# Issuing more of a routed-expert kernel's list loads from GpSimd: 239 of its transfers in place of 211

## The chip, the cores and the metric

The kernel runs on one core of a Trainium2 chip. A core has a matrix engine (PE in the profile, its weight loads PEld), a vector engine (DVE), a scalar engine (ACT), a general-purpose engine (GpSimd, POOL in the profile) and a sync engine (SP) that only issues transfers. Each engine has its own queue of instructions and runs it in order; engines meet at semaphores. Transfers (DMAs) are issued by SP, ACT or GpSimd, and all share 16 DMA engines. Those issued by SP and ACT appear in the profile as "hardware dynamic", those issued by GpSimd as "software dynamic".

The metric is the device time of one execution in microseconds (us). The median of three runs before the change is 696.01 us, with 694.29 and 697.36 at the ends.

## What is computed

The first half is a gated linear recurrence over 768 steps for 4 x 8 heads of size 48. Its result, 3072 rows of 384 numbers, is the input of the second half, a mixture of 8 experts in which every row goes to the two experts with the highest noisy score. Everything is 32-bit floating point.

```python
for t in range(S):
    state = alpha[:, :, t, :, None] * state + np.einsum('bhd,bhe->bhde', k[:, :, t], v[:, :, t])
    y[:, :, t] = np.einsum('bhd,bhde->bhe', q[:, :, t], state)
...
noisy_logits = logits + noise_scale * noise
top2 = np.argpartition(-noisy_logits, 2, axis=1)[:, :2]
...
for e in range(E):
    for k in range(2):
        mask = top2[:, k] == e
        h = np.maximum(x[mask] @ w1[e], 0.0)
        out[mask] += top2_w[mask, k, None] * (h @ w2[e])
```

## The kernel before

**Recurrence.** It is done in 24 chunks of 128 steps with matmuls and scans. Each chunk's rows go to a table `x_rows` in device memory (`put_rows`). Beside the chunks and, later, beside the first expert tiles, a routing takes place in four units of six chunks: it picks the two experts of each row and writes one list entry of four words for each choice into a `table` in device memory: row number, gate, the other expert, and the rank in the other expert's list. An entry of expert e with rank r lies in row e * 3072 + r. The entries are written by 48 indirect transfers issued by GpSimd (`put_entries`, L161), 12 for each unit.

**Expert tiles.** Rows are then worked off in 24 pairs of 128-row tiles (`pairs`), and three half tiles of 64 rows (`half_tiles`). Pairs 0 to 7 are the first 256 entries of the experts 0 to 7; pairs 8 to 23 are the second and third 256 entries, two pairs for an expert, from expert 7 down. Pairs are multiplied with a seven-product scheme in place of eight products; the sums that it needs are made by DVE. For each pair there are these steps:

- `load_tab`: the 256 list entries, 4 KB as 256 runs of 16 bytes, into `tab` (6 buffers). Line 1017 decides who issues it: SP for pairs 0 to 13, GpSimd from pair 14 on (`PLANNED` = 14). From pair 14 on the place of the list in the table is read from a `plan` that the routing's last steps compute (`of_plan`).
- `load_w1`, `load_w2`: 1.5 MB each, only where the expert is new; issued by SP.
- `find_rows` (DVE) turns the entries into row numbers, `gather` (GpSimd, L886, two indirect transfers) brings the rows of `x_rows`, `turn_x` transposes them.
- `get_prev` (GpSimd, L871, two indirect transfers) brings what an earlier tile has written for the same rows to the output; it waits for all earlier output writes. `combine` (DVE, L1155) adds, and `put_pair` (GpSimd, L879, two indirect transfers) writes the output.

A half tile has the same steps with one indirect transfer each; `load(j)` (L1260) reads its place from the plan, loads its 64 entries through SP (L1263) and then both weights.

`take_tile` makes a list load wait for the entries that it may read: those of the first two units for pairs 0 to 7, all 48 writes for later pairs and half tiles.

**Order.** There is no scheduler: `steps(i)` gives every step of pair i a time on a common axis on which a pair takes 20 units, and the list of all steps is sorted by it and emitted in that order, for every engine. On this axis `load_tab(i)` lies at 20i - 32, `find_rows` at 20i - 27, `gather` at 20i - 26, `get_prev` at 20i + 8.5, `combine` at 20i + 20.9 and `put_pair` at 20i + 22.2; a half tile's `load` lies 48 units before its base. So `load_tab(i)` stands, on the queue of whoever issues it, just ahead of `get_prev(i-2)`. The entries' writes of the last unit end at 126.3.

**Transfers of GpSimd before.** 48 entry writes, 48 gathers, 48 loads and 48 writes of earlier output for pairs, 9 for half tiles, and 10 list loads: 211. A transfer of 128 rows is spread over the 16 DMA engines, 8 rows on each; a list load of a pair puts 16 runs on each, one of a half tile's transfers 4. Completion of each transfer is counted on one of eight semaphores that GpSimd's transfers take in turn; SP's take turns over eight others.

**End.** After the last output write, branches on two counts skip code for rare cases (L1406 and L1408), GpSimd waits for its transfers, and the program ends with a drain of every engine (line 1443, the end of the launch).

Of the kernel before, what the change touches and what calls it, by code (L numbers as in the profile page):

```python
# [9 lines left out]
F32 = mybir.dt.float32  # L10
# [8 lines left out]
def kernel(  # L19
# [32 lines left out]
    nc = tc.nc  # L52
    B, H, S, D = q.shape
    N, DM = out.shape
    E, _, F = moe_w1.shape
    C = 128
# [8 lines left out]
    NU = NT // UC  # L65
    LEVELS = [1 << i for i in range(C.bit_length() - 1)]
    HC = C // 2
# [5 lines left out]
    TROWS = E * RMAX + (E + 0) * C  # L73
# [3 lines left out]
    R2 = 2 * C  # L77
# [68 lines left out]
    table = dram.tile([TROWS, 4], U32, name="table")  # L146
# [22 lines left out]
    def take_tile(get, units=NU):  # L169
        count = 1 + 2 * UT // C * units  # L170
        for put in entries[:count]:
            tc.add_manual_dep(get.ins, put.name, AFTER, reason="reads any row of the table that these fill")
        for put in entries[count:]:
            tc.declare_no_dep(get.ins, put, reason="rows behind those of the tile")
        taken.append(get.ins)
# [694 lines left out]
    def get_rows(rows, at):  # L870
        get = nc.gpsimd.indirect_dma_start(out=rows.bitcast(U32), out_offset=None, in_=out.bitcast(U32),  # L871
                                           in_offset=bass.IndirectOffsetOnAxis(ap=at, axis=0),
                                           bounds_check=N - 1, oob_is_err=False)
        for put in order["puts"]:
            tc.add_manual_dep(get.ins, put.name, AFTER, reason="reads rows of any earlier tile")
        order["gets"].append(get.ins)
# [8 lines left out]
    def get_x(rows, at, units):  # L885
        nc.gpsimd.indirect_dma_start(out=rows, out_offset=None, in_=x_rows[0:units * UT, :],  # L886
                                     in_offset=bass.IndirectOffsetOnAxis(ap=at, axis=0),
                                     bounds_check=units * UT - 1, oob_is_err=False)

    def of_plan(i, what, most, engine=mybir.EngineType.SP):  # L890
        return nc.values_load(plan[0:1, i, what:what + 1], engines=[engine], min_val=0, max_val=most,
                              skip_runtime_bounds_check_because=WHY)

    def load_weights(e, w1, w2):
        if w1 is not None:
            nc.sync.dma_start(out=w1, in_=moe_w1[ds(e, 1)].rearrange("o (a p) f -> p (o a) f", p=C))
        if w2 is not None:
            nc.sync.dma_start(out=w2, in_=moe_w2[ds(e, 1)].rearrange("o (a p) d -> p (o a) d", p=C))

    def choose_rows(on, tab, where, i):  # L900

        R = tab.shape[0]
        skip, second, before_it = tab[:, 4:6], tab[:, 6:7], tab[:, 7:8]
        other = on["two"].tile([C, E], F32, name="other")[0:R]
        nc.vector.scalar_tensor_tensor(other, expert_ids[0:R], tab[:, 2:3], given[0:R, i, 0:E], op0=ALU.is_equal,
                                       op1=ALU.mult, accum_out=before_it)
        nc.vector.memset(skip[:, 0:1], 0.0)
        nc.vector.tensor_tensor(skip[:, 1:2], tab[:, 3:4], before_it, op=ALU.is_ge)
        nc.vector.tensor_tensor(second, tab[:, 3:4], before_it, op=ALU.is_lt)
        nc.vector.scalar_tensor_tensor(where, skip, float(NONE), tab[:, 0:1].to_broadcast([R, 2]),  # L910
                                       op0=ALU.mult, op1=ALU.add)
# [77 lines left out]
    PLANNED = E + 2 * AFTER_GROUP[0]  # L989
# [4 lines left out]
    def pairs(on):  # L994
# [14 lines left out]
        tabs, wheres, weights, bank = {}, {}, {}, {}  # L1009
# [4 lines left out]
                nc.gpsimd.memset(t, 0.0)  # L1014

        def load_tab(i):
            by, engine = (nc.gpsimd, mybir.EngineType.Pool) if i >= PLANNED else (nc.sync, mybir.EngineType.SP)
            row = order_of[i] * RMAX + [0, R2, 2 * R2][rounds[i]] if i < PLANNED else of_plan(FIRST_PAIR + i - E, 1, TROWS - R2, engine)
            tabs[i] = on["tab"].tile([C, 2, 8], F32, name="tab")
            take_tile(by.dma_start(out=tabs[i][:, :, 0:4],  # L1020
                                        in_=table.bitcast(F32)[ds(row, R2), :].rearrange("(s p) w -> p s w", p=C)),
                      2 if i < E else NU)

        def load_w1(i):
            if is_new[i]:
# [216 lines left out]
    def half_tiles(on, places, shared):  # L1242

        one = on["one"]
        flat = places.rearrange("p n h d -> p (n h d)")
        w1 = flat[:, 0:KO * F].rearrange("p (a f) -> p a f", a=KO)
        w2 = shared[:, 0:FO * DM].rearrange("p (f d) -> p f d", f=FO)
        x_in = one.tile([C, DM], F32, name="x_half")[0:HC]
        prev = one.tile([C, DM], F32, name="prev_half")[0:HC]
        xt = one.tile([C, KO, HC], F32, name="xt_half")  # L1250
        h_rows = flat[:, KO * F:KO * F + HF]
        h = flat[:, KO * F + HF:KO * F + 2 * HF].rearrange("p (f t) -> p f t", t=C)
        o = one.tile([C, DM], F32, name="o_half")[0:HC]
        tabs, wheres = {}, {}

        def clear_rows():
            for t in (x_in, prev):
                nc.gpsimd.memset(t, 0.0)

        def load(j):  # L1260
            row, e = of_plan(j, 1, TROWS - C), of_plan(j, 0, E - 1)
            tabs[j] = on["tab"].tile([C, 8], F32, name="tab_half")[0:HC]
            take_tile(nc.sync.dma_start(out=tabs[j][:, 0:4], in_=table.bitcast(F32)[ds(row, HC), :]))  # L1263
            load_weights(e, w1, w2)

        def find_rows(j):
            wheres[j] = on["tab"].tile([C, 2], U32, name="where_half")[0:HC]
            choose_rows(on, tabs[j], wheres[j], j)

        def gather(j):  # L1270
            get_x(x_in, wheres[j][:, 0:1], NU)

        def turn_x(j):
            x_ps = on["tp"].tile([C, KO, C], F32, tag="tp", name="x_ps")[:, :, 0:HC]
            for a in range(KO):
                nc.tensor.transpose(x_ps[:, a, :], x_in[:, ds(a * C, C)], ident[0:HC, 0:HC])
            nc.scalar.copy(xt, x_ps)

        def layer1(j):
            h_ps = on["y"].tile([C, HF], F32, tag="y", name="h_half_ps")  # L1280
            for a in range(KO):
                for g in range(2):
                    nc.tensor.matmul(h_ps[ds(g * HC, HC), :], xt[:, a, :], w1[:, a, ds(g * HF, HF)],  # L1283
                                     start=a == 0, stop=a == KO - 1, skip_group_check=True)
            nc.scalar.activation(h_rows, h_ps, AF.Relu)

        def turn_h(j):
            h_ps = on["y"].tile([C, FO // 2, C], F32, tag="y", name="h_half_ps")
            for f in range(FO // 2):
                nc.tensor.transpose(h_ps[:, f, :], h_rows[:, ds(f * C, C)], ident)  # L1290
            nc.scalar.copy(h, h_ps)

        def layer2(j):
            ps = on["y"].tile([C, DM], F32, tag="y", name="half_ps")
            for f in range(FO // 2):
                for g in range(2):
                    nc.tensor.matmul(ps[ds(g * HC, HC), :], h[:, f, ds(g * HC, HC)], w2[:, g * FO // 2 + f, :],  # L1297
                                     start=f == 0, stop=f == FO // 2 - 1, skip_group_check=True)
            nc.scalar.copy(o, ps[HC:C])
            nc.vector.tensor_tensor(o, o, ps[0:HC], op=ALU.add)  # L1300
            nc.scalar.activation(o, o, AF.Copy, scale=tabs[j][:, 1:2])

        def combine(j):
            nc.vector.scalar_tensor_tensor(prev, prev, tabs[j][:, 6:7], o, op0=ALU.mult, op1=ALU.add)

        def steps(j, base):
            return [(base + t, go) for t, go in (
                (-48.0, lambda: load(j)), (-36.0, lambda: find_rows(j)), (-32.1, lambda: gather(j)),
                (-19.9, lambda: turn_x(j)), (-10.15, lambda: layer1(j)), (-0.05, lambda: turn_h(j)),
                (10.4, lambda: layer2(j)),  # L1310
                (8.5, lambda: get_rows(prev, wheres[j][:, 1:2])), (12.9, lambda: combine(j)),
                (13.4, lambda: put_tile(prev, wheres[j][:, 0:1])))]

        return steps, clear_rows
# [133 lines left out]
```

## Time and profile before

| what | value |
|---|---|
| median of three runs | 696.01 us (694.29 to 697.36) |
| the profiled execution, its own time | 710.9 us |
| its span, first to last instruction | 709.2 us |
| granted clock of the matrix engine, mean | 0.983 |
| busy: DVE, ACT, POOL | 455.0, 260.3, 300.4 us |
| packets of GpSimd's transfers | 11504, 23.76 MB |
| packets of SP's transfers | 134132, 80.41 MB |

The profiled execution is 14.9 us longer than the median of the others. Its steps are read on its own clock, from the start of its span. "Busy" leaves out register, branch and semaphore instructions and drains; those stand in the trace as work of an engine's sequencer (POOLq for that of GpSimd). A group line such as `L1020 POOL DMA_DIRECT2D tab<-table x10: 775/788/800` gives the source line, the engine, the operation, what is written from what, the count, and the shortest, median and longest duration in ns.

The recurrence takes the first 165 us or so, the pairs the rest, to 692 us. In the pairs the matrix engine takes 19.9 us for a pair.

### The profile page before, as it was taken

What the parts mean: (1) busy time and instruction counts of PE and PEld (TensorE: products, weight loads), DVE (VectorE), ACT (ScalarE), POOL (GpSimd) and SP (SyncE); (2) the same over time, 40 slices, a digit from 0 to 9 for tenths busy, and PEclk for the clock granted to TensorE, in tenths of its full rate; (3) what the DMA queues carried; (4) which work ended last, traced back from release to release, by engine and by line L of the source; (5) the groups of instructions that cost most, each with busy time, mean ns of one, the idle gap of its engine ahead of it and who ended that gap; (6) DMA issues with size and microseconds to landing.
All of it is one profiled execution on the core that took longest, in us unless ns stands there. A gap on an engine that the chain in (4) does not pass through costs nothing.

```text
span 709.2 us, 15155 instructions
## 1 busy us (share of the span) xinstructions
PE 675.1 (95%) x5777; PEld 628.9 (89%) x5777; DVE 455.0 (64%) x1058; ACT 260.3 (37%) x561; POOL 300.4 (42%) x390
## 2 busy tenths in 40 slices
PE   7999999999999997999999999999999999999990
PEld 5888877878999997989999999988999889999890
DVE  8777867856778774877466667464565646645440
ACT  4456545444443323222333332333332233323330
POOL 5442483764234573586322335412453224533121
PEclk9999999999999998999999999999999999999996
DMA  9777576567866754575413457137351574521110
GB/s 177 169 154 156 129 135 136 127 129 212 285 201 221 224 150 129 198 198 189 141 37 123 136 193 261 54 130 271 117 199 60 174 251 135 157 60 38 32 45 24
DMA packets 145861, 105.64 MB, mean 149 GB/s; under 512 B 110931, under 2 KB 133151, under 8 KB 145780
## 3 DMA queue, kind: packets, MB, share of 16 engines
q1 hardware_dynamic: 134132, 80.41, 40.8%
q0 software_dynamic: 11504, 23.76, 10.8%
q8 instruction: 48, 0.79, 0.5%
q10 hardware_dynamic: 144, 0.41, 0.2%
q14 instruction: 33, 0.27, 0.1%
HBM read 95.19 MB, written 14.96 MB: 155 GB/s over the span
## 4 chain that ended last, share of the span: by engine, by line
PE 53%; issue 6%; POOL 1%; another core or an unknown queue 1%; ACT 1%; DMA 1%; DVE 0%; POOLq 0%; ACTq 0%; DVEq 0%
PE sc L1127 22%; PE o_ps L1134 13%; PE h_ps L1134 10%; PE h_ps L1127 4%; PE x_ps L1065 2%; PE half_ps L1297 1%; PE h_half_ps L1283 1%; DMA out_dram<-prev,where 1%; POOL out_dram L879 0%; POOL prev L871 0%; POOL x_in L886 0%; ACT L651 0%; ACT m L1205 0%; ACT m L1203 0%
## 5 line engine op out<-in xcount | busy, mean ns | idle before, releaser
L886 POOL DMA_INDIRECT x_in<-x_rows,where x48 | 52.6, 1095 | 138.0 <-PE h_ps L1134 87.8
L871 POOL DMA_INDIRECT prev<-out_dram,where x48 | 54.1, 1127 | 67.4 <-issue 29.6
L1127 PE MATMUL sc<-xs,ws 128*128 128x128 f32 x576 | 74.5, 279 | 2.2 <-ACT m L1205 1.9
L879 POOL DMA_INDIRECT out_dram<-prev,where x48 | 51.7, 1076 | 58.7 <-DVE prev L1155 43.3
L1127 PE MATMUL sc<-xt,w 128*128 128x128 f32 x576 | 73.9, 279 | 0.0
L1127 PEld LDWEIGHTS sc<-xs,ws 128*128 128x128 f32 x576 | 69.1, 194 | 3.1 <-ACT m L1205 2.5
L1134 PE MATMUL o_ps<-wt,hx 128*128 128x192 f32 x384 | 70.6, 327 | 0.2 <-issue 0.2
L1127 PEld LDWEIGHTS sc<-xt,w 128*128 128x128 f32 x576 | 70.8, 196 | 0.0
L1138 ACT ACTIVATE h<-h 128x512 f32<-128x512 f32 x72 | 45.4, 631 | 64.1 <-DVE h L1074 60.9
L1074 DVE TENSOR_TENSOR h<-sc,m 128x512 f32<-128x512 f32 x48 | 33.1, 692 | 50.0 <-PE sc L1127 45.1
L1134 PEld LDWEIGHTS o_ps<-wt,hx 128*128 128x128 f32 x384 | 63.5, 190 | 0.9 <-issue 0.5
L161 POOL DMA_INDIRECT table<-entry,place_u x48 | 53.0, 1105 | 15.9 <-issue 14.6
L1127 PE MATMUL sc<-xs,w 128*128 128x128 f32 x384 | 49.3, 282 | 1.2 <-DVE h L1074 1.2
L1127 PEld LDWEIGHTS sc<-xs,w 128*128 128x128 f32 x384 | 44.9, 192 | 4.8 <-DVE h L1074 3.8
L369 POOL TENSOR_TENSOR k_P<-k_P,over 128x512 f32<-128x512 f32 (+1 forms) x25 | 28.8, 1153 | 47.8 <-DVE over L353 36.5
L1127 PE MATMUL h_ps<-xt,w 128*128 128x128 f32 x384 | 47.1, 276 | 0.0
L326 PE MATMUL tp<-ident,ins 128*128 128x128 f32 x288 | 42.9, 285 | 4.0 <-issue 2.9
L1127 PEld LDWEIGHTS h_ps<-xt,w 128*128 128x128 f32 x384 | 44.8, 192 | 0.2
L1143 ACT ACTIVATE o<-o_ps,tab 128x192 f32<-128x192 f32 x23 | 9.6, 419 | 96.0 <-PE o_ps L1134 86.1
L345 DVE TENSOR_TENSOR_SCAN P_all<-shared,least 128x516 f32<-128x516 f32 (+1 forms) x25 | 30.3, 1216 | 17.8 <-ACT shared L340 9.5
L1074 DVE TENSOR_TENSOR h<-h_ps,m 128x512 f32<-128x512 f32 x24 | 16.6, 691 | 36.9 <-PE h_ps L1127 33.5
L326 PEld LDWEIGHTS tp<-ident,ins 128*128 128x128 f32 x288 | 31.4, 143 | 9.2 <-issue 4.0
(235 smaller groups left out, 1411.9 us busy)
## 6 DMA issues: line engine op xcount, KB each, us to landing
w<-in_moe_w_dram SPq DMA_DIRECT2D x30, 1536.0 KB
ins<-in_alpha_dram SPq DMA_DIRECT2D x24, 192.0 KB
ins<-in_k_dram SPq DMA_DIRECT2D x24, 192.0 KB
ins<-in_q_dram SPq DMA_DIRECT2D x24, 192.0 KB
vt<-in_v_dram SPq DMA_DIRECT2D x24, 192.0 KB
x_rows<-y_sb SPq DMA_DIRECT2D x24, 192.0 KB
ins<-in_moe_w_dram SPq DMA_DIRECT2D x3, 1536.0 KB
shared<-in_moe_w_dram SPq DMA_DIRECT2D x3, 1536.0 KB
```

The source lines that it names most:

```text
L161: put = nc.gpsimd.indirect_dma_start(out=table, out_offset=bass.IndirectOffsetOnAxis(ap=place, axis=0), in_=entry, in_offset=None, bounds_ ...
L326: nc.tensor.transpose(tp[:, j, :], src[:, 2 * j:2 * j + 2, :], ident)
L345: nc.vector.tensor_tensor_scan(P_all[:, at], a_all[:, at], least.rearrange("p j t -> p (j t)")[:, at], 0.0, op0=ALU.mult, op1=ALU.max)
L369: nc.gpsimd.tensor_tensor(c["k"][:, at], c["k"][:, at], over[:, at, 1:CB], op=ALU.mult)
L871: get = nc.gpsimd.indirect_dma_start(out=rows.bitcast(U32), out_offset=None, in_=out.bitcast(U32), in_offset=bass.IndirectOffsetOnAxis(ap= ...
L879: put = nc.gpsimd.indirect_dma_start(out=out, out_offset=bass.IndirectOffsetOnAxis(ap=at, axis=0), in_=rows, in_offset=None, bounds_check= ...
L886: nc.gpsimd.indirect_dma_start(out=rows, out_offset=None, in_=x_rows[0:units * UT, :], in_offset=bass.IndirectOffsetOnAxis(ap=at, axis=0), ...
L1065: nc.tensor.transpose(x_ps[:, a, :], x_in[i % 2][:, s, ds(a * C, C)], ident)
L1074: nc.vector.tensor_tensor(to, p, q, op=ALU.add)
L1127: nc.tensor.matmul(bank[name][:, f, :], W[:, ds(f * C, C)], X, start=new and f == 0, stop=True, skip_group_check=True)
L1134: nc.tensor.matmul(bank[name], H[:, f, :], W[:, f, :], start=new and f == 0, stop=True, skip_group_check=True)
L1138: nc.scalar.activation(t, t if src is None else src, AF.Relu)
```

## The change

The list loads of pairs 2, 3 and 4 and of pairs 8 to 13 move from SP to GpSimd, as do those of the three half tiles, with the reading of their place in the plan. From pair 8 on each list load is issued as two transfers of 128 entries. The loads of pairs 0, 1, 5, 6 and 7 stay with SP. What is loaded, and what each load waits for, is the same. GpSimd's transfers become 211 + 3 + 12 + 10 + 3 = 239.

```diff
         def load_tab(i):
-            by, engine = (nc.gpsimd, mybir.EngineType.Pool) if i >= PLANNED else (nc.sync, mybir.EngineType.SP)
+
+            by, engine = (nc.sync, mybir.EngineType.SP) if i < 2 or 5 <= i < E else (nc.gpsimd, mybir.EngineType.Pool)
             row = order_of[i] * RMAX + [0, R2, 2 * R2][rounds[i]] if i < PLANNED else of_plan(FIRST_PAIR + i - E, 1, TROWS - R2, engine)
             tabs[i] = on["tab"].tile([C, 2, 8], F32, name="tab")
-            take_tile(by.dma_start(out=tabs[i][:, :, 0:4],
-                                        in_=table.bitcast(F32)[ds(row, R2), :].rearrange("(s p) w -> p s w", p=C)),
-                      2 if i < E else NU)
+            parts = 1 if i < E else 2
+            for s in range(parts):
+                take_tile(by.dma_start(out=tabs[i][:, ds(s, 2 // parts), 0:4],
+                                       in_=table.bitcast(F32)[ds(row + s * C, R2 // parts), :].rearrange("(s p) w -> p s w", p=C)),
+                          2 if i < E else NU)
...
         def load(j):
-            row, e = of_plan(j, 1, TROWS - C), of_plan(j, 0, E - 1)
+            row, e = of_plan(j, 1, TROWS - C, mybir.EngineType.Pool), of_plan(j, 0, E - 1)
             tabs[j] = on["tab"].tile([C, 8], F32, name="tab_half")[0:HC]
-            take_tile(nc.sync.dma_start(out=tabs[j][:, 0:4], in_=table.bitcast(F32)[ds(row, HC), :]))
+            take_tile(nc.gpsimd.dma_start(out=tabs[j][:, 0:4], in_=table.bitcast(F32)[ds(row, HC), :]))
             load_weights(e, w1, w2)
```

## The prediction

> **What bounds the kernel now.** I read the stretches first, then the matrix engine's waits, then what follows its last product. The columns of the stretches are: from and to, length, busy time of PE, PEld, DVE, ACT and POOL with counts, granted clock, DMA share, GB/s.
>
> ```profile
> 340.00:400.00 60.00, 60.00 (x455) 59.46 (x454) 38.40 (x101) 19.78 (x39) 18.91 (x18) 1.00 0.34 107
> 400.00:500.00 100.00, 100.00 (x731) 94.98 (x731) 59.82 (x151) 32.62 (x65) 33.94 (x33) 1.00 0.50 169
> 500.00:600.00 100.00, 100.00 (x748) 94.98 (x747) 56.47 (x137) 34.65 (x69) 39.60 (x38) 1.00 0.46 148
> 600.00:692.00 92.00, 92.00 (x668) 86.86 (x666) 48.54 (x118) 28.67 (x57) 29.03 (x27) 1.00 0.24 77
> 692.00:710.00 18.00, 0.01 (x1) 0.00 (x0) 0.80 (x3) 0.00 (x0) 2.02 (x2) 0.59 0.07 23
> ```
>
> From 340 to 692 us the matrix engine has no gap. All list loads whose form the change touches, but those of pairs 2 to 4 and 8, are used in there: nothing that arrives earlier can shorten it. The median of the runs is 14.9 us below this execution's 710.9, about the gaps before 340, so an undisturbed run should have still fewer. What is left to win lies behind 692: 17 us without a product. Two listings by line tell what GpSimd's sequencer does there, and at the start (count, shortest/median/longest ns, first and last start):
>
> ```profile
> L1443 POOLq DRAIN  x3: 46/103/8652, 699.7 to 708.9; - x3
> ...
> L1408 POOLq INC_SWDGE_SEM  x1: 2287/2287/2287, 697.4 to 697.4; - x1
> ...
> L1432 POOLq DRAIN  x1: 188/188/188, 0.5 to 0.5; - x1
> ```
>
> The last output writes are issued at 692.10 and 693.42 and their packets end in the 696th us. Then one drain of GpSimd takes 8.65 us while every other engine waits. Before any transfer had been issued, the same instruction took 0.19 us. It is the largest item at the end, and it belongs to the engine that the change gives 28 more transfers.
>
> GpSimd's timeline has one gap that no wait explains. Between the two halves of a pair's `prev` loads there are otherwise 0.30 us:
>
> ```profile
> 380.13 1.04 POOL L871 DMA_INDIRECT prev<-out_dram,where  x1 [2.43 <-DMA out_dram<-prev,where]
> 381.48 1.01 POOL L871 DMA_INDIRECT prev<-out_dram,where  x1 [0.30 <-issue]
> ...
> 402.27 1.04 POOL L871 DMA_INDIRECT prev<-out_dram,where  x1 [5.40 <-DMA out_dram<-prev,where]
> 405.44 1.02 POOL L871 DMA_INDIRECT prev<-out_dram,where  x1 [2.13 <-DVE hx L1071]
> ```
>
> I counted what each of the 16 DMA engines has got from GpSimd by then: 8 row descriptors and one for the semaphore for a transfer of 128 rows (9), 4 + 1 for one of a half tile (5), 16 + 1 for a list load (17). The transfer at 402.27 ends at 1017, that at 405.44 would end at 1026. So the gap of 2.13 - 0.30 = 1.83 us lies where the count passes 1024.
>
> [...] list loads that SP issues right behind a weight load landed 7.2 to 8.3 us after issue here (pairs 2 to 5), with no weights ahead after 2.0 to 2.5 us (pairs 0, 1, 8 to 10). [...]
>
> **The change, part by part.**
>
> *The ring.* Before: 192 transfers of 128 rows x 9 = 1728, 9 of half tiles x 5 = 45, 10 lists x 17 = 170; sum 1943, which is once round and 919 into the second lap. After: pairs 2 to 4 add 3 x 17 = 51, pairs 8 to 13 add 6 x 2 x 9 = 108, pairs 14 to 23 add 10 x (18 - 17) = 10, half tiles add 3 x 5 = 15. The sum is 2127: twice round and 79 slots. [...] the drain is the only candidate in the trace with a price. If it works through what the current lap has used, it costs (8.65 - 0.19) / 919 = 9.2 ns a slot, and after the change 0.19 + 79 x 0.0092 = 0.92 us: 7.73 less. If it depends on nothing: 0. If it goes with all slots: 8.46 x 184 / 1943 = +0.80. I take the first: [...] a drain with nothing used was short. The semaphore instruction ahead of it (2.29) I leave as it is.
>
> *A second passing.* The first moves from pair 10's `prev` load to the gather of pair 10 (1023 before it), with 8.7 us of idle ahead of it at 369.47; the second falls on the last half tile's output write (2045 before it, 666.49). 1.83 us there delays the `prev` loads of pair 22 (669.38, 670.72), which land some 2.6 us after issue, to about 675.1; `combine` runs at 676.14. Cost 0, with 1 us left; beyond that DVE has 2.8 us of idle (before 680.11).
>
> *Issue time.* A direct list load takes 0.788 us on GpSimd:
>
> ```profile
> L1020 POOL DMA_DIRECT2D tab<-table x10: 775/788/800, 439.2 to 628.6; - x10
> ...
> SPq L1020 <- DMA table<-entry,place_u: 20.2, 6, 11.1
> ```
>
> One of half the size isn't in the trace: between half, 0.39, and 0.79 each; I take 0.79. 28 more are 22 us of GpSimd, and it is busy 300 of 709. They stand ahead of `get_prev(i-2)`, which waits for the last output writes to land. For pairs 14 on, the second part (0.79) fits into waits of 1.4 to 1.8 us ahead of it (441.40: 1.39); for pairs 9 to 13 two parts, 1.6 us, into 2.4 to 6.6 (343.67 to 424.24). Pair 4's load has 0.63 us of idle ahead of the `prev` load at 230.85, used at 243: 0.2 us late, nobody waits. Half tiles' loads come after `prev` loads, some 10 us ahead of their `find_rows`, against 2.1 to 6.3 us for the landing of GpSimd's list loads in the trace. Cost 0.
>
> *Pair 8, the one new wait on the path of others.* Its load needs all 48 entry writes. SP bore that (11.1 us above, with only weights behind it for which nobody waits). Now GpSimd bears it:
>
> ```profile
> 324.25 0.97 POOL L161 DMA_INDIRECT table<-entry,place_u  x1 [0.31 <-issue]
> 325.94 1.49 POOL L871 DMA_INDIRECT prev<-out_dram,where  x1 [0.71 <-issue]
> 327.73 1.40 POOL L871 DMA_INDIRECT prev<-out_dram,where  x1 [0.31 <-issue]
> ```
>
> The last entry landed at 327.53. Two parts go out by 329.2, the `prev` loads of pair 6 at 329.5 and 330.9, 3.2 to 3.6 us later than before. Landed after 2.1 to 3.8 us, undisturbed, that is 333.0 to 334.7, and `combine` of pair 6 ran at 334.19. The list lands at 330.6 to 332.3; `find_rows` of pair 8 ran at 331.56. So DVE waits 0 to 1 us. Behind it stands the sum that frees nothing before 340.92, with 3.43 us of DVE idle: the matrix engine doesn't see it. SP, freed of that wait, can issue weights of pair 10 some 5 us earlier than 329.14, into the same stretch; a `prev` load under such traffic took up to 9.7 us, so this cover can fail. I take 0.2 us, range 0 to 3.
>
> *SP.* 12 list loads fewer; nothing waits for SP's issuing. 0.
>
> Sum: -7.73 + 0.2 = -7.5. The profiled execution goes from 710.9 to about 703.4, the median from 696.01 to 688.5, if the end is the same without the profiler.
>
> **The rivals.** A difference under 0.5% (3.5 us) is about what a measurement of this kernel can't tell from none.
>
> *R1, the drain has a fixed price* (or goes with all slots). For: nothing in one trace shows its dependence[...]. Against: 0.19 us at the start. Then all is hidden: 696 to 697.
>
> *R2, the drain fills up the lap* to come back to slot 0: 105 slots were left, so 8.46 / 105 = 81 ns a slot, and 945 are left after: 76.3, +67.7 us, 764 us. It decides as soon as the count passes 2048. Against: no packet of GpSimd's queue runs after 697.
>
> *R3, the drain is fixed and GpSimd comes too late at pair 6/8:* `prev` loads issued at 330.9 and landing after 9.7 us, at 340.6, hold `combine` 6 us, past DVE's 3.43 us; with the loss of the first transposes behind that, and a second passing on the last half tile that has only 1 us of cover, 3 to 5 us: 700. It decides from a landing at 337.6 on. Against: typical landings are half of that.
>
> **How the numbers follow.** Main case 0.64: 688.5, its own range 686 (semaphore instruction too) to 691.5 (pair 6 late by 3). R1 0.20: 694.5 to 697.5. R3 0.10, R2 0.06. Holding the main case and R1 gives 686 to 697.5, with 0.16 and tails left out. Faster 0.64, same 0.20, slower 0.16.
>
> **What would show it.** Right: the longest drain in line 1443's listing near 0.9 us, no gap in the products from 340 on, an unexplained GpSimd gap of about 1.8 us ahead of pair 10's gather and the last half tile's write. A drain still at 8.7 is R1, one of tens of us R2. A DVE wait for `prev` at 334 to 340 and a product gap behind it is R3. The forecast is wrong if the drain doesn't shrink, or if the runs without a profiler don't have it.

## The result and the profile after

The changed kernel takes 690.82 us (median of 11 runs, 688.51 to 693.94), the kernel before beside it 694.31 us (691.67 to 697.78). The ratio is 0.9943, 95% interval 0.9919 to 0.9967: 4.0 us less (2.3 to 5.6); the two medians differ by 3.5. Forecast were 7.5 us less, 688.5 us. The ratios of this document leave out runs more than 1.5% above the fastest run of their kernel: none here and in the first eight experiments, but in one comparison on another chip half of the runs of the kernel before, so that the ratios there say little.

The profile of before that the prediction worked from (710.9 us, span 709.2 us) was longer than all 11 runs timed beside the changed kernel. The kernel before was profiled again for the experiments, at a span of 696.7 us, and the changed kernel, at 688.1 us, is read against that one. It too is no typical execution: its time, 698.42 us, is the longest of its 22 runs.

First the end of the program. The listings of the last drain and of the semaphore instruction ahead of it, changed kernel (count, shortest/median/longest ns, first and last start):

```profile
L1446 POOLq DRAIN  x3: 46/103/2031, 685.3 to 687.8; - x3
...
L1411 POOLq INC_SWDGE_SEM  x1: 672/672/672, 684.6 to 684.6; - x1
```

The drain fell from 8652 to 2031 ns, the semaphore instruction from 2287 to 672: 6.62 + 1.62 = 8.24 us less, while no other engine has work. Behind the last product the program now lasts 8.9 us (679.2 to 688.1) in place of 18.0 (678.7 to 696.7); of these 9.1 us, 0.9 are the landing of the last output write, 5.2 us after the last product here and 6.1 there. So the gain at the end was larger than the forecast as a whole, and some 4.3 us (8.24 - 3.96; 2.6 to 5.9) were lost ahead of it. This 4.3 is what is left over between the times and the end; it isn't measured by itself.

The last products of the two profiles, at 679.2 and 678.7, seem to show no such loss. But the execution profiled as before was late from the start: in the profiles of the changed kernel and of the first eight experiments the products stop at 180.5 us, for 1.0 to 4.7 us (1.9 in the changed kernel, 4.2 in this one), and its pair 0 comes 4.7 us later. Distances between the same product of different pairs (`o_ps<-w,h`, the first with the second weights) leave this out. From pair 8 to the last product both kernels take 327.5 us. From pair 6 to pair 8 the changed kernel takes 46.3 us and the kernel before 40.3. The product in pairs 6 and 8, changed kernel first (start and duration, us):

```profile
305.40 1.47 PE L1137 MATMUL o_ps<-w,h 128*128 128x192 f32 x8
351.66 1.47 PE L1137 MATMUL o_ps<-w,h 128*128 128x192 f32 x8
...
310.88 1.47 PE L1134 MATMUL o_ps<-w,h 128*128 128x192 f32 x8
351.15 1.47 PE L1134 MATMUL o_ps<-w,h 128*128 128x192 f32 x8
```

So the loss lies between pairs 6 and 8, and is 6.0 us in this profile, just above the interval.

What it looks like, the stretches show (from and to, length, busy time of PE, PEld, DVE, ACT and POOL with counts, granted clock, DMA share, GB/s). The kernel before, profiled again:

```profile
320.00:325.00 5.00, 5.00 (x45) 4.97 (x45) 3.77 (x7) 1.67 (x4) 3.84 (x4) 1.00 1.01 402
325.00:330.00 5.00, 5.00 (x45) 4.85 (x44) 1.45 (x3) 2.30 (x4) 0.58 (x1) 1.00 1.03 355
330.00:335.00 5.00, 5.00 (x36) 5.00 (x35) 3.92 (x11) 2.20 (x5) 2.45 (x2) 1.00 0.16 47
```

The changed kernel:

```profile
310.00:320.00 10.00, 10.00 (x78) 9.97 (x77) 2.84 (x5) 2.15 (x4) 3.23 (x4) 1.00 0.79 262
320.00:325.00 5.00, 3.03 (x28) 2.83 (x26) 4.25 (x14) 0.49 (x2) 2.58 (x2) 1.00 0.21 60
325.00:330.00 5.00, 3.97 (x18) 3.97 (x19) 2.96 (x5) 1.40 (x3) 3.22 (x5) 0.54 0.42 136
330.00:335.00 5.00, 5.00 (x28) 5.00 (x27) 2.70 (x10) 2.30 (x5) 2.21 (x2) 0.78 0.14 41
335.00:340.00 5.00, 5.00 (x33) 5.00 (x32) 1.58 (x8) 0.42 (x1) 2.00 (x2) 1.00 0.42 118
340.00:400.00 60.00, 60.00 (x454) 59.47 (x454) 40.67 (x107) 19.77 (x39) 23.12 (x24) 1.00 0.29 92
400.00:500.00 100.00, 100.00 (x748) 94.99 (x747) 57.28 (x137) 34.49 (x68) 40.11 (x42) 1.00 0.52 174
500.00:600.00 100.00, 100.00 (x739) 95.13 (x738) 59.11 (x156) 32.29 (x64) 43.03 (x45) 1.00 0.52 174
```

From 330 us to the last product the matrix engine is busy throughout: GpSimd issues 28 half lists there (pairs 10 to 23) in place of 10 whole ones, and three loads of half tiles, and nothing is late. The loss is a hole at 323 to 326, and a clock granted at 0.54 and 0.78 behind it. DVE was idle before that, busy for 2.84 of the 10 us from 310 on. What it waited for is in its timeline; the changed kernel (start, length, line, operation, and in brackets the idle time ahead of it with its releaser):

```profile
312.44 0.95 DVE L1074 TENSOR_TENSOR wt<-w,wt 128x768 f32<-128x768 f32 x1
320.64 0.17 DVE L1046 TENSOR_SCALAR tab<-tab 128x2 f32<-128x2 f32 x1 [7.26 <-DMA tab<-table]
...
325.31 1.27 DVE L1077 TENSOR_TENSOR h<-sc,m 128x512 f32<-128x512 f32 x2
```

The matrix engine's timeline of the same kernel:

```profile
321.08 1.95 PE L1130 MATMUL sc<-xt,w 128*128 128x128 f32 x16
326.03 3.78 PE L1130 MATMUL sc<-xs,w 128*128 128x128 f32 x16 [3.00 <-DVE h L1077]
```

DVE stands for 7.26 us at `find_rows` of pair 8, the first reader of pair 8's list. The sums `h` that free the matrix engine's accumulators are queued behind it, so the products stand for 3.00 us, and the next 16 take 3.78 us (2.05 where they don't stand, below). The list in turn was late because GpSimd waited for the last entry writes; GpSimd's timeline, changed kernel:

```profile
306.89 1.37 POOL L161 DMA_INDIRECT table<-entry,place_u  x1 [0.30 <-issue]
314.39 1.15 POOL L1023 DMA_DIRECT2D tab<-table  x2 [6.13 <-DMA table<-entry,place_u]
```

The write issued at 306.89 has landed at 313.73 by its last semaphore count, the one before it (305.39) at 312.66: 6.8 and 7.3 us after issue. In the kernel before, profiled again, the same two took 3.4 and 3.2 us. The two halves of the list, issued at 314.39 and 314.96, take 5.7 and 5.6 us to land. So pair 8's list is late for two reasons: the writes that it waits for land late, and then it does so itself. The prediction had GpSimd wait for these writes, but took their landing from the old profile, 3.3 us after issue, and had the list landed 3.1 to 4.8 us after them; here it is 6.8.

### The profile page after: what moved, and what is told of

Its sections match the earlier page's. It is cut to its first block, busy times and chain, and to the rows that moved or that the text cites. A ratio compares the mean times of both kernels' runs of the same rounds, so it can differ in the third digit from the quotient of the medians.

```text
span 688.1 us, 15191 instructions
## 1 busy us (share of the span) xinstructions
PE 671.0 (98%) x5777; PEld 628.8 (91%) x5777; DVE 455.3 (66%) x1058; ACT 260.1 (38%) x561; POOL 319.9 (46%) x418
## 5 line engine op out<-in xcount | busy, mean ns | idle before, releaser
L1130 PE MATMUL sc<-xs,ws 128*128 128x128 f32 x576 | 73.1, 276 | 0.0
L1130 PE MATMUL sc<-xt,w 128*128 128x128 f32 x576 | 72.2, 275 | 0.0
L1130 PEld LDWEIGHTS sc<-xt,w 128*128 128x128 f32 x576 | 69.1, 192 | 0.0
L161 POOL DMA_INDIRECT table<-entry,place_u x48 | 54.4, 1133 | 16.0 <-issue 15.0
L1130 PE MATMUL sc<-xs,w 128*128 128x128 f32 x384 | 51.0, 288 | 4.9 <-DVE h L1077 4.9
L1130 PEld LDWEIGHTS sc<-xs,w 128*128 128x128 f32 x384 | 46.3, 197 | 8.6 <-DVE h L1077 6.5
L1074 DVE TENSOR_TENSOR hx<-h,hx 128x512 f32<-128x512 f32 x24 | 16.6, 693 | 33.9 <-ACT h L1141 33.8
```

The costliest lines, as they stand in the source:

```text
L161: put = nc.gpsimd.indirect_dma_start(out=table, out_offset=bass.IndirectOffsetOnAxis(ap=place, axis=0), in_=entry, in_offset=None, bounds_ ...
L1074: nc.vector.tensor_tensor(to, p, q, op=ALU.subtract)
L1130: nc.tensor.matmul(bank[name][:, f, :], W[:, ds(f * C, C)], X, start=new and f == 0, stop=True, skip_group_check=True)
```

## The experiments

All are compared with the kernel before, run beside them. The first eight ran on one chip, on which the kernel before takes 694 us; the last four on two others, on which it takes 715 and 716 us. The chip of the result above isn't on record; the kernel before took 694 us there too.

**The kernel before, once more.** No edit. It tries whether the drain's 8652 ns and the place of GpSimd's pause were an accident of one execution.

> The kernel before, once more, for a second profile of it. Theory 'ring position' (the last drain's length follows the slots used in the current lap of 1024): 919 slots used again, so the drain is 8.0 to 9.0 us again and the semaphore instruction ahead of it 2 us or more. Theory 'accident' (the long drain belongs to the one disturbed profile of 710.9 us): the drain is 2 us or less. Ratio 1.00.

Measured: ratio 1.0006 (0.9988 to 1.0024), drain 8652 ns, semaphore instruction 2287 ns, both to the nanosecond what they were, and the unexplained gap of 2.13 us again ahead of transfer 114. So neither is an accident. Below, such a gap is called a pause; the recorded texts call it a passing or a start over. That GpSimd's transfers go round a ring in laps of 1024 slots was an assumption of mine, which no run shows; shown is a pause between counts of 1017 and 1026. The count is made of what each of the 16 DMA engines gets: in the trace of the kernel before, an entry write is 16 packets of 128 bytes (8 entries of 16 bytes) and 16 of 4 bytes, a list 16 of 256 bytes and 16 of 4.

**The count alone.** The kernel before, with 20 transfers on GpSimd that nothing reads (231 in all), all lists where they were.

```diff
+        extra = const.tile([C, 24, E], F32, name="extra")
+
+        def more_transfers(k):
+            nc.gpsimd.dma_start(out=extra[:, k, :], in_=moe_noise[ds(k * C, C), :])
+
+        spots = [T * i + 8.2 for i in range(6, 22)] + [T * i + 10.0 for i in range(8, 12)]
...
+                       [(t, lambda k=k: more_transfers(k)) for k, t in enumerate(spots)],
```

> The kernel before, all list loads as they were, and 20 more transfers of GpSimd of 128 rows each, from an input into a tile that nobody reads: 231 transfers, 2123 slots, 75 used of the third lap. Ring position: drain 1.5 to 2.5 us, 6 to 7 us less than before, and no wait of DVE for a list of pair 8, so faster than the changed kernel: ratio 0.985 to 0.991. 'Moving the lists is what helps': no list moves, so the drain and the time stay or the time grows by the 16 us of added GpSimd work where it shows: ratio 1.00 to 1.01.

Measured: ratio 0.9902 (0.9868 to 0.9936). The drain in the listing of this kernel:

```profile
L1450 POOLq DRAIN  x3: 46/103/2118, 684.9 to 687.5; - x3
```

Twenty useless transfers make the program 6.8 us faster. The semaphore instruction takes 692 ns. So the time at the end follows what GpSimd has issued, and not which list goes where: no list moved.

**Pair 8's list back on SP.** The changed kernel, with that one list issued by SP in one piece (237 transfers).

```diff
-            by, engine = (nc.sync, mybir.EngineType.SP) if i < 2 or 5 <= i < E else (nc.gpsimd, mybir.EngineType.Pool)
+            by, engine = (nc.sync, mybir.EngineType.SP) if i < 2 or 5 <= i <= E else (nc.gpsimd, mybir.EngineType.Pool)
...
-            parts = 1 if i < E else 2
+            parts = 1 if i <= E else 2
```

> The changed kernel with pair 8's list alone back on SP, in one transfer: 2109 slots, 61 used of the third lap. Theory 'two effects' (the short drain gains 6.6 to 8 us, and pair 8's list on GpSimd loses 3 to 5 us by a wait of DVE and a gap of the products at 322 us): drain 1.5 to 2.2 us, no DVE wait for the list of pair 8 over 1 us, no product gap at pair 7/8; ratio to before 0.985 to 0.991, 2 to 4 us under the changed kernel. Rival 'that gap is an accident of the profile, the rest of the gain is missing because the drain is shorter without a profile': time as the changed kernel, ratio 0.993 to 0.996.

Measured: ratio 0.9892 (0.9864 to 0.9919), 685.66 us, drain 1867 ns. DVE's wait for the list is 1.5 us, a little over the 1 us expected, and the products have no gap from 183 us on; from pair 6 to pair 8 they take 40.3 us. So the loss goes when this one list goes back, and the gain at the end stays.

**Whole lists of pairs 8 to 13 on GpSimd and nothing else** (217 transfers).

```diff
-            by, engine = (nc.gpsimd, mybir.EngineType.Pool) if i >= PLANNED else (nc.sync, mybir.EngineType.SP)
+            by, engine = (nc.gpsimd, mybir.EngineType.Pool) if i >= E else (nc.sync, mybir.EngineType.SP)
```

> Lists of pairs 8 to 13 on GpSimd, one transfer each, everything else as before: 217 transfers, 2045 slots, 1021 used and 3 left of the second lap. Ring position, used slots: drain 9 to 10 us, and pair 8's wait of DVE is there, so slower: ratio 1.003 to 1.010. Rival 'slots left' (the drain fills the lap up): drain under 1 us, ratio 0.990 to 0.996.

Measured: ratio 0.9926 (0.9908 to 0.9945), drain 1302 ns. The expectation missed: I had counted this kernel to end just ahead of a second pause, and it has it at transfer 210, seven before its last: GpSimd is idle for 3.52 us there, up to 658.16, where it is for 2.12 and 1.79 in the two kernels below. My count of slots stands at 1973 by then, below twice the 1017 of the first pause. The loss at pair 8 is there too, without half lists, half tiles or early pairs: DVE waits 8.3 us for the list, the products stand for 4.0 us and take 46.0 us from pair 6 to pair 8. End -9.15 us, whole -5.1 us, so 4.0 us lost (2.8 to 5.3).

**No list on GpSimd** (201 transfers): line 1017 as above with the condition `i < 0`.

> Every list of a pair issued by SP: 201 transfers of GpSimd in place of 211. Theory A (GpSimd's last drain is 0.64 us and the semaphore instruction after it 0.34 us, and both grow with the number of transfers since the ring last started over, together 0.101 us a transfer): the start over stays at transfer 114, 88 transfers follow it, drain 7.8 us, semaphore instruction 2.1 us, 1.0 us off the end, ratio 0.9985 (0.995 to 1.001). Theory B (GpSimd's own work in the later pairs is what costs the time, so that taking all lists from it is the gain): drain may be anything, ratio below 0.993. Theory C (an end's cost by all transfers of the launch): drain 8.2 us.

Measured: ratio 0.9969 (0.9949 to 0.9989), drain 7833 ns, semaphore instruction 2095 ns. Theory A's figures, to 0.03 us; B and C fall.

**Lists of pairs 10 to 13 on GpSimd**: the same condition as `i >= 10` (215 transfers).

> The kernel before with the lists of pairs 10 to 13 on GpSimd as well, in one part each, those of pairs 8 and 9 on SP as before: 215 transfers. Theory A: the second start over lies near transfer 212, some 4 transfers follow, drain 0.97 us and semaphore instruction 0.42 us, 9.5 us off the end; no wait of VectorE for the list at pair 8 and no product gap of 3 us there; ratio 0.986 (0.984 to 0.990), lower than the 0.9926 with pairs 8 and 9 on GpSimd. Rival (the loss comes from any early list on GpSimd, not from pair 8's place right behind the entry writes): ratio 0.991 to 0.993 as in the run from pair 8, with a wait for a list at pair 10.

Measured: ratio 0.9861 (0.9818 to 0.9904), drain 1057 ns, semaphore instruction 432 ns, the second pause at transfer 211 (a gap of 1.90 us), no wait of DVE for a list. With pairs 8 and 9 left to SP the loss is gone; the lists of pairs 10 to 13 cost nothing that shows by being issued by GpSimd.

**Lists of pairs 11 to 13 on GpSimd**: `i >= 11` (214 transfers).

> As the one from pair 10, with the lists of pairs 11 to 13 alone moved: 214 transfers. The start over falls on the last one or two transfers, or is not reached. If it is reached: drain 0.7 to 0.8 us, semaphore instruction 0.36 to 0.38 us, 9.7 us off the end, less the stall of about 1.8 us of the start over, which now stands in the last writes of the output where nothing hides it: ratio 0.986 to 0.989. If it is not reached: 101 transfers since transfer 114, drain 8.9 us, semaphore instruction 2.3 us, ratio 1.000 to 1.002. The two are 8 us apart by three small transfers less or more.

Measured: ratio 0.9847 (0.9809 to 0.9885), 684.36 us, semaphore instruction 392 ns. The second pause is reached, one transfer earlier than expected, so drain and semaphore instruction lie a little above the ranges given for it, and the ratio a little below. The drain in the listing of this kernel:

```profile
L1443 POOLq DRAIN  x3: 46/103/893, 684.7 to 686.1; - x3
```

The last two loads of earlier output in its GpSimd timeline:

```profile
668.35 1.04 POOL L871 DMA_INDIRECT prev<-out_dram,where  x1 [2.42 <-DMA out_dram<-prev,where]
671.35 1.12 POOL L871 DMA_INDIRECT prev<-out_dram,where  x1 [1.96 <-issue]
```

The second pause comes with transfer 212 of 214 and is 1.96 - 0.30 = 1.66 us long. It delays the very last load, but the next output write (678.55) comes 6 us later, and the time shows no price. This version and the two with ratios 0.986 and 0.989 beat both kernels: their intervals end at 0.9885, 0.9904 and 0.9919, where that of the changed kernel begins. They overlap, so none of the three is the best one.

**Pair 8's list alone on GpSimd**: `i == E or i >= PLANNED` (212 transfers).

> The kernel before with pair 8's list alone moved to GpSimd, in one part: 212 transfers, no second start over. Theory A: drain 0.64 + 99 x 0.0817 = 8.7 us and semaphore instruction 2.3 us, as before; what is left is the loss of pair 8's list: VectorE waits 6 to 7 us for it, the products stand for 3 us and then run at half clock, 3.8 to 4.5 us: ratio 1.005 to 1.007 (1.003 to 1.009). Rival (pair 8's list costs nothing by itself, and what the change lost it lost in the halves or in the half tiles): ratio 0.999 to 1.001.

Measured: ratio 1.0011 (0.9983 to 1.0040), drain 8815 ns. Here my theory of the loss fell: the list that costs 4 us in the changed kernel costs nothing that shows when it moves alone (40.4 us from pair 6 to pair 8). Its rival doesn't fit either, since the run with whole lists lost 4 us without any half. The timelines tell the difference. SP's timeline with pair 8's list alone on GpSimd:

```profile
312.03 0.88 SPq L1020 DMA_DIRECT2D tab<-table  x2
313.07 0.37 SPq L896 DMA_DIRECT2D w<-in_moe_w_dram  x1
314.78 0.37 SPq L898 DMA_DIRECT2D w<-in_moe_w_dram  x1
```

SP's timeline of the changed kernel:

```profile
304.94 0.37 SPq L896 DMA_DIRECT2D w<-in_moe_w_dram  x1
313.40 0.37 SPq L898 DMA_DIRECT2D w<-in_moe_w_dram  x1
```

GpSimd's timeline with pair 8's list alone:

```profile
308.83 1.41 POOL L161 DMA_INDIRECT table<-entry,place_u  x1 [0.30 <-issue]
312.67 0.77 POOL L1020 DMA_DIRECT2D tab<-table  x1 [2.43 <-DMA table<-entry,place_u]
```

DVE's timeline of that kernel:

```profile
317.59 0.17 DVE L1043 TENSOR_SCALAR tab<-tab 128x2 f32<-128x2 f32 x1 [2.82 <-DMA tab<-table]
```

Its matrix engine, at the place of the hole:

```profile
324.45 2.05 PE L1127 MATMUL sc<-xs,w 128*128 128x128 f32 x16
```

Where SP still has a list of pair 8, 9 or 10, it waits with it for the entry writes, and pair 10's weights (L896, L898, 1.5 MB each) stand behind it on SP's queue until 313. Where it has none, the first weights go out at 305, while the last entry writes are on their way: 6.1 us of waiting against 2.4.

The closest comparison is with the run from pair 8 on, whole. GpSimd issues the same transfers in the same order in both kernels, pair 8's list as a whole among them, up to the list of pair 9, which it has there and issues at 329 us, behind the hole. Before that only SP differs: there it has none of the lists of pairs 9 and 10. GpSimd's and SP's timelines of that kernel:

```profile
307.72 1.42 POOL L161 DMA_INDIRECT table<-entry,place_u  x1 [0.30 <-issue]
315.18 0.77 POOL L1020 DMA_DIRECT2D tab<-table  x1 [6.05 <-DMA table<-entry,place_u]
...
305.22 0.37 SPq L896 DMA_DIRECT2D w<-in_moe_w_dram  x1
```

From 308 to 311 us the DMA engines are busy for 0.99 of the time there, and for 0.14 with pair 8's list alone on GpSimd. The last two entry writes land 7.7 and 6.7 us after issue there, and 3.2 and 3.1 here.

Every run beside a kernel before of 694 us falls in line: the changed kernel and the one with whole lists from pair 8 on (none of 8 to 10 on SP) have their last two entry writes landed after 6.7 to 7.7 us, take 46.3 and 46.0 us from pair 6 to pair 8 and lose 4 us; the seven others leave SP one or more of these lists, have them landed after 2.5 to 3.7 us, take 40.3 to 40.4 us, and lose nothing that can be measured. That SP's freed queue is behind the loss is shown by this; that the weights on their way slow the entry writes is the reading that fits the doubled landing times and the DMA share of 0.99 against 0.14. How the DMA engines divide their time between the two, no run here shows.

**SP held again.** To try the weights' part directly, the changed kernel got a second load of pair 8's list through SP, which nothing reads and behind which the weights have to wait. Pair 8's own list stays with GpSimd.

```diff
+            if i == E:
+                spare = one.tile([C, 2, 4], F32, name="spare")
+                take_tile(nc.sync.dma_start(out=spare, in_=table.bitcast(F32)[ds(row, R2), :].rearrange("(s p) w -> p s w", p=C)))
             parts = 1 if i < E else 2
```

> The changed kernel with one more transfer: SP loads pair 8's list a second time, into a tile that nothing reads. Pair 8's list itself stays with GpSimd. Theory W (the loss at pair 8 comes from SP: without lists of its own it no longer waits for the entry writes, so it issues pair 10's first weights at 305 us in place of 313 to 317, and these slow the last two entry writes from 3.1 to 7 us): SP is held again, the weights go out near 313 us, the last two entry writes land 3 to 3.7 us after their issue, VectorE's wait for the list falls from 7.3 us to under 3.5, the product gap of 3.0 us at 326 goes, ratio 0.988 to 0.990. Rival G (pair 8's list costs this because GpSimd issues it, with its waits, between the entry writes and the loads of pair 7): nothing changes, ratio 0.9935 to 0.995.

> The changed kernel with SP held by a second load of pair 8's list, once more, since on the chip of the last comparison the products ran some 20 us later and pair 10's weights came behind the entry writes in every kernel. Where the kernel before takes 694 us: theory W as before, weights near 313 us, the last two entry writes landed 3 to 3.7 us after their issue, VectorE's wait for the list under 3.5 us, no product gap of 3 us at 326, ratio 0.988 to 0.990; rival G: list wait 6 to 8 us and gap 3 us stay, ratio 0.9935 to 0.995. Where it takes 714 us: weights after 320 us with or without the hold, so that neither theory is tried, ratio 0.992 to 1.000.

Measured: 0.9958 (0.9921 to 0.9994), and on the other chip 0.9799 (0.9732 to 0.9865). One kernel with two results that exclude each other says nothing of half a per cent, and the case to be tried didn't arise: on both chips the products come later, and the buffer for these weights isn't free before the entries have landed. Wherever no list holds them back, the weights go out 0.5 to 1.0 us before pair 6's product `o_ps<-w,h`, at 305 us in the two kernels that lost 4 us and at 324 to 331 on these two chips. With the hold they go out at 330 us:

```profile
324.41 0.37 SPq L1023 DMA_DIRECT2D spare<-table  x1
330.27 0.37 SPq L896 DMA_DIRECT2D w<-in_moe_w_dram  x1
```

**The kernel before with early weights.** Pair 10's first weights ahead of pair 8's list on SP.

```diff
-                (at("tab", -32.0), lambda: load_tab(i)), (at("w1", -29.5), lambda: load_w1(i)), (at("w2", -19.8), lambda: load_w2(i)),
+                (at("tab", -27.0 if i == E else -32.0), lambda: load_tab(i)), (at("w1", -67.5 if i == E + 2 else -29.5), lambda: load_w1(i)), (at("w2", -19.8), lambda: load_w2(i)),
```

> The kernel before, all lists of pairs 8 to 13 on SP, with the first weights of pair 10 put ahead of pair 8's list in SP's order. Theory W: these weights go out near 305 us, the last two entry writes land about 7 us after their issue in place of 3.2, pair 8's list 3 to 4 us later, VectorE waits 1 to 5 us for it; drain 8.65 us as before; ratio 1.001 to 1.006 (the second weights stay behind the lists, so less than the 0.0065 that the changed kernel lost). Rival G: entry writes land in 3.2 us, ratio 0.999 to 1.001.

Measured: 1.0009 (0.9967 to 1.0051), drain 8652 ns. The weights left at 328 us, behind the last entry writes, for the same reason. So the early weights were not tried here either.

**The changed kernel again**, beside these.

> The changed kernel as it is, beside the one with SP held: ratio 0.992 to 0.997, drain 2.03 us, the wait of VectorE for pair 8's list 7.3 us and the product gap 3.0 us in the same place. If the wait or the gap is gone, they were an accident of one execution and the difference between the kernels has another cause.

Measured: 0.9916 (0.9888 to 0.9945), drain 2031 ns to the nanosecond. DVE's wait for pair 8's list isn't there, and neither are the early weights:

```profile
324.00 0.37 SPq L896 DMA_DIRECT2D w<-in_moe_w_dram  x1
332.46 0.37 SPq L898 DMA_DIRECT2D w<-in_moe_w_dram  x1
```

The last two entry writes, issued at 317.38 and 318.65, meet no weights, and GpSimd issues pair 8's list 2.8 us after them, at 322.38, against 6.1 us in the first profile. The products do stop, for 3.7 us at 316.6, but a pair earlier and without a list to wait for; the kernel before with early weights stops in the same place, also for 3.7 us. From pair 6 to pair 8 the four profiles of these chips take 40.6 to 41.0 us: no loss. I had expected wait and gap in the same place and called their absence a sign of an accident. With the runs of the other chip, where wait and early weights come and go together, the nearer reading is that both depend on when the weights' buffer comes free; it fits, but an experiment that sets the weights' time alone is missing.

**The end, all runs together.** n is the number of GpSimd's transfers from its last pause to the end, the one behind the pause included:

| kernel | transfers | n | drain, ns | semaphore instruction, ns | ratio |
|---|---|---|---|---|---|
| lists from pair 11 on GpSimd | 214 | 3 | 893 | 392 | 0.9847 |
| from pair 10 | 215 | 5 | 1057 | 432 | 0.9861 |
| from pair 8, whole | 217 | 8 | 1302 | 492 | 0.9926 |
| changed, pair 8 on SP | 237 | 15 | 1867 | 632 | 0.9892 |
| changed | 239 | 17 | 2031 | 672 | 0.9943 |
| before, 20 useless ones | 231 | 18 | 2118 | 692 | 0.9902 |
| no list on GpSimd | 201 | 88 | 7833 | 2095 | 0.9969 |
| before | 211 | 98 | 8652 | 2287 | 1 |
| pair 8's list alone | 212 | 100 | 8815 | 2327 | 1.0011 |

The first and last rows give (8815 - 893) / 97 = 81.7 ns of drain for each transfer and 893 - 3 x 81.7 = 648 ns besides; all others lie within 7 ns of that line. For the semaphore instruction the same two rows give 19.9 ns and 332 ns. On the other chips the kernels with 239 and 211 transfers have the same 2031 and 8652 ns. The times of the runs have it too, not only the profiles: against before, drain and semaphore instruction together fall by 9.7, 9.5, 8.4 and 8.1 us in the four versions with a second pause and no loss at pair 8, and these are 10.6, 9.7, 7.5 and 6.8 us faster (from pair 11, from pair 10, changed with pair 8 on SP, 20 useless transfers), each inside its interval.

## Why the prediction was right, and where not

*The bound and the end.* Right. The products had no gap from 330 us on, and the only thing to win lay behind the last of them. The drain grows with the transfers since the last pause, by 81.7 ns each; R1 (fixed, or with all slots) and R2 (filling the lap up) fall with the table above. The laps of 1024, from which the forecast's 79 slots come, were an assumption; from the first pause alone, between counts of 1017 and 1026, and laps of equal length, the same sum would have given an estimate of 0.87 to 1.05 us. The second pause, at 1973, doesn't bear out equal laps of slots counted like this.

*The size of the drain.* Forecast 0.92 us, measured 2.03. Of the difference 0.46 is the constant, for which the prediction took the 0.19 us of a drain without any transfer ahead of it and which is 0.65. The other 0.65 is the place of the second pause: forecast at the last half tile's output write, with 79 slots or some 9 transfers left to the end, found with 17 left, between the halves of a list (changed kernel, GpSimd):

```profile
615.80 0.60 POOL L1023 DMA_DIRECT2D tab<-table  x1
618.93 0.57 POOL L1023 DMA_DIRECT2D tab<-table  x1 [2.54 <-issue]
620.14 1.06 POOL L871 DMA_INDIRECT prev<-out_dram,where  x1 [0.63 <-issue]
```

The price was right: 9.2 ns a slot with 9 slots to a transfer is 83 ns, against 81.7. In part that is luck: the constant was taken too small, which makes the price too high, and whole lists were counted as nearly two transfers, which makes it too low. That it goes by transfers, the prediction didn't have: ten whole lists, which it counted as 17 slots each, separate the rows of 88 and 98 and add 819 ns, 82 each, as any transfer does. Which of the slot counts was too small, the runs don't settle.

*The semaphore instruction.* "I leave as it is" was the second wrong term: it shrinks with the same n, by 1.62 us. The two together are 8.24 us off the end, against 7.73 forecast.

*Issue time.* Half a list takes 0.57 to 0.61 us on GpSimd, between the two bounds and under the 0.79 taken. The covers held, the second pause included: 0, as forecast. (The first can't be seen in the changed kernel; where it was forecast, ahead of pair 10's gather at 359.3, GpSimd stands for 11.2 us anyway.)

*Pair 8.* This is the step that failed. It was costed at 0.2 us with a range of 0 to 3; the runs show 4.3 us (2.6 to 5.9) for the changed kernel, and its profile 6.0. The prediction saw that SP, freed of its wait, could issue pair 10's weights earlier into the same stretch, and asked only what that does to the `prev` loads of pair 6. It took the landing of the entries, 327.53 in that profile, as given. But that landing was measured while SP's wait held the weights back. With the wait gone, the entries were late first (the last two landed 7.3 and 6.8 us after issue, against 3.2 and 3.4 in the kernel before), the list next, and DVE with everything queued behind `find_rows`. R3 named the right place, GpSimd late at pair 6 and 8, and the right engine behind it, but a wait for `prev` in place of one for the list, and it came with the smaller drain and not in place of it. The profile that the prediction read was of no help here: its pairs 0 to 6 take 131.6 us, against 120.5 to 121.5 in the profiles of the changed kernel and of the first eight experiments, and 135.6 to 141.1 on the two slower chips, where the loss doesn't occur.

*The sum.* Forecast -7.73 + 0.2 = -7.5; measured -8.24 + 4.3 = -4.0, where 4.3 is the remainder. Two errors of opposite sign and unequal size, inside the range. That 690.8 us lies even in the main case's own range, 686 to 691.5, is luck: counted from the 696.01 us that it started from, this range says 4.5 to 10 us less, and the kernel before took 694.3 beside the changed one. The chance for faster went to the right item, the drain.

## What to carry to other kernels

When a wait is taken off a queue, list what stood behind it on that queue and will now start earlier, and ask which transfers of the old profile had a clear road only because of that wait; their landing times may not be carried over (here 3.2 and 3.4 us became 7.3 and 6.8). What an instruction at the end of a program costs can depend on a count that the whole program runs up (here a drain of 893 to 8815 ns): compare it across kernels with different counts before taking it as fixed. And the stop of the matrix engine cost more here than its length: 16 products took 3.78 us behind a hole of 3.00, at a granted clock of 0.54, against 2.05 without one, and the hole of 3.00 cost 6.0 us in all.

## What the runs showed of the hardware

GpSimd's last drain and the semaphore instruction ahead of it cost 0.65 + 0.33 us and 0.0817 + 0.0199 us for each of its transfers since its last pause; nine kernels with 3 to 100 such transfers fit, with drains of 893 to 8815 ns, and ten whole lists add 819 ns, 82 each. A pause is a gap that no wait in the profile explains: 2.13 us in the kernel before, 1.90 and 1.96 in those with the lists from pair 10 and from pair 11, 2.54 in the changed one, where there are otherwise 0.3 or none. It holds GpSimd's next transfer by 1.6 to 2.5 us. What brings it about, the runs don't show: the first comes between counts of 1017 and 1026, the second before twice that, at 1973 in the kernel with whole lists from pair 8. Twenty useless transfers shortened the program by 6.8 us: with them 18 transfers follow the last pause in place of 98, and the drain takes 2118 ns in place of 8652.

Two chips ran the same program 3% slower than a third, with the products stopped elsewhere (pairs 0 to 6 took 135.6 to 141.1 us against 120.5 to 121.5), and the loss of 4 us on the one wasn't found on the others. A profile and the times that it is to explain belong on one chip.
